# Block 6's first product by seven half-size products, first block's stores at once, another load order: a retention-plus-MLP kernel on one Trainium2 core

## The chip, the cores and the metric

The kernel runs on one core of a Trainium2 chip. Its time is device microseconds of one execution; lower is better. The engines are TensorE (PE in the profile, with its weight loads as PEld), VectorE (DVE), ScalarE (ACT), GpSimd (POOL) and SyncE (SP). Each works through its own instructions in order, and semaphores make one wait for another. POOL issues the loads (software queue, q0); SP issues the transposing DMAs and the stores (hardware queue, q1). Both queues are worked off by the same 16 DMA engines.

## The reference

```python
def _attn_ref(q, k, v):                      # (8, 8, 576, 64) each
    scores = scale * np.matmul(q, k.transpose(0, 1, 3, 2))
    gamma = 1.0 - 2.0 ** (-5.0 - np.arange(H))
    rel = pos[:, None] - pos[None, :]
    Dmat = np.where(rel >= 0, gamma[:, None, None] ** rel, 0.0)
    return np.matmul(scores * Dmat, v)
def _moe_ref(x, w_in, w_out):                # w_in 512 x 2048, w_out 2048 x 512
    h = x @ w_in
    g = 0.5 * h * (1.0 + erf(h * inv_sqrt2))
    return g @ w_out
# reference: x = attention's output, tokens first, 4608 x 512; then _moe_ref
```

There is no softmax, so the decay mask can be split into a factor of the row, a factor of the column and a running state between chunks of 128 positions.

## The kernel before, in words

**Attention.** The 8 batches are cut into chunks of 128 positions (the last has 64). One chunk of one batch is a unit of 128 tokens; there are 36 units in 22 groups (a group is two batches' units at the same chunk, or one unit of two 64-row tails; the first four groups are single units). In this text g4, g13, g17 and so on are groups by number; g7, g11, g16 and g21 are the short ones. For each group q and k are loaded with a cast to bf16, turned (q and k transposed), and then come: scores (`sc`, L507, L516, L526), a masked product on DVE (`ret`, L545, L549), `inner` (`o_ps`, L582, L591), `state` (`u_ps`, L610), `cross` (`o_ps` with `u_sb`, L642), and `evacuate` (L661), which writes the unit's tokens into `xT`. The first seven groups are turned by TensorE (L478); g7 to g21 by two transposing DMAs each on SP (`qkT<-qk_ld`, L489; `turn_dma`), one for q and one for k. TensorE's score matmuls of a group stand in its order and wait for both.

**MLP.** Nine blocks of 512 tokens, four units each. The first product (`mlp1`, `hT`, L690) of blocks 0 to 6 takes 64 matmuls of 128x128 on 512 columns per block; ACT applies Gelu (L699). The second product of block 0 is plain (`mlp2`, `oT`, L735); those of blocks 1 to 8 use seven half-size products instead of eight (`part`, `m`, L874, 112 matmuls of 256 columns per block), with sums on DVE (`sum_g`, L771 to L775) and combinations in `after`. Blocks 7 and 8 take seven products for the first product too (`fast`, `f`, L955, 112 matmuls of 256 columns): `sum_in` and `sum_last` (L913 to L920) make sums of `w_in` once, `sum_x` (L928) makes four sums of a block's `xT`, and each of the seven products goes through copies and additions on ACT and DVE (L452, L457, L970, L974) before Gelu (L976, L980).

**Order.** The order of all instructions is written at build time by a list scheduler inside the kernel: it keeps an estimated clock for each engine and for the two DMA queues and always issues the first piece whose inputs it believes ready. `ORDER` gives the load order of the first loads, and with it delays and choices found by search: `s20+3.0` keeps unit 20's group from being scored until 3.0 us after the believed landing of its transposes, `b6+0.3` does the same for `inner`, and `a8` puts the scaling of unit 8's v on ACT. Later loads follow group by group. `FAST` is the first block whose first product is done by seven products.

**Queues.** The four stores of block 0 are kept in `kept_back` and go out one at a time behind later transposes, from `HOLD` groups on:

```python
def store_kept():
    if kept_back and nD >= HOLD:
        store(*kept_back.pop(0))
```

`turn_dma` emits both transposes of a group when both its q and k are believed landed. POOL's loads are issued in order, at most eight in flight; a load waits also for its buffer (five pairs of q and k).

Of the kernel before, what the change touches and what calls it, by code (L numbers as in the profile page):

```python
# [17 lines left out]
def kernel(  # L18
# [14 lines left out]
    nc = tc.nc  # L33
# [19 lines left out]
    groups = [[0], [1], [2], [3]]  # L53
# [6 lines left out]
    N_U = len(units)  # L60
    group_of = {i: n for n, g in enumerate(groups) for i in g}
# [6 lines left out]

    N_PE_TR = 7
    HW_FIRST = ((("q", 0),), (("k", 0),))  # L70
    FAST, ALL_FAST = 7, 7
    N_LD = 5
    N_QKT = 4
    N_VH = 6
# [2 lines left out]
    A_TURNS = 2  # L77
    HOT = 5.3
    N_WARM = 10
    HOLD = 9  # L80

    const = ctx.enter_context(tc.tile_pool(name="const", bufs=1))
    ld_pool = ctx.enter_context(tc.tile_pool(name="ld", bufs=1))
# [176 lines left out]
    def hw_dma(issue, work, ready, put=lambda end: None, shares=TURN_SHARES):  # L260
        at = max(T["sp"], ready)
        if len(hw_flying) >= 3:
            T["sp"] = max(T["sp"], hw_flying[-3]["end"])
        T["sp"] = max(T["sp"], at + issue)
        hw_flying.append(transfer(1, at, work, put, shares))
# [59 lines left out]
    for x, keys in enumerate(zip(*HW_FIRST)):  # L325
        for n, (what, i) in enumerate(keys):
            land[what, i] = (4.6, 5.2)[n] + 0.75 * x
            t = tiles_of(i)
            cast_due[what, i] = (t[1] if what == "v" else t[0][:, "qk".index(what)], first[what, i])
    ORDER = ("wi1 q1 k1 wi0 io q2 k2 v0 v1 q3 wi2 v2 wi3 k3 wi4 v3 q4 wi5 wi6 q5 k4 a8 dq2 k5 wo1 wi7 wo0 v5 v4 "  # L330
# [4 lines left out]
             "b22+3.0 s23+2.0 s15+0.3 s13+3.0").split()  # L335

    BY_ACT = {int(x[1:]) for x in ORDER if x[0] == "a"}
    S_LATE = {int(x[1:].split("+")[0]): float(x.split("+")[1]) for x in ORDER if x[0] == "s"}
# [142 lines left out]
        release(b, done + 0.05)  # L481
        sg[n]["T"] = max(sg[n].get("T", 0.0), done + SEM)

    def turn_dma(n):
        qk, qkT = loaded[groups[n][0]][0], qkT_of(n)
        short = units[groups[n][0]][2] is None
        rows = TAIL if short else C
        for jj in range(2):
            nc.sync.dma_start(qkT[:, jj, :, 0:rows], qk[0:rows, jj].rearrange("p h j d -> p (h j d)"), transpose=True)  # L489
            ends = sg[n].setdefault("ends", {})  # L490

            def put(end, jj=jj):
                ends[jj] = end
                sg[n]["T"] = max(ends.values()) + SEM

            hw_dma(1.3, MOVE["turn"] * (0.62 if short else 1.0), max(land["qk"[jj], i] for i in groups[n]), put)

    def scores(n):
        g = groups[n]
# [215 lines left out]
    def store(t, ts, src, lo=0, hi=d_model, *on_queues):  # L715
        for x, (row, p0, n) in enumerate(rows_of(t, ts)):
            queue = on_queues[x] if on_queues else nc.sync
            queue.dma_start(out[row:row + n, lo:hi], src[p0:p0 + n])
        for _ in rows_of(t, ts):
            hw_dma(0.4, MOVE["store"] * (hi - lo) / d_model / len(rows_of(t, ts)), max(T["act"], T["dve"]), putter(o_free, (t, ts // 2)), STORE_SHARES)  # L720
# [7 lines left out]
    def mlp2(t, ts, m0, m1):  # L728
        cols = slice(ts * 128, ts * 128 + 128)
        if m0 == 0:  # L730
            acc[t, ts] = bank([128, d_model], FP32, "oT")
        b, oT = acc[t, ts]
        pe_waits(max(max(land_out[m // 2] + SEM, g_at[t, m, ts]) for m in range(m0, m1)))
        for m in range(m0, m1):
            nc.tensor.matmul(oT, lhsT=g_of(t, m // 2)[:, m % 2, cols], rhs=w_out_sb[m // 2][:, m % 2, :],  # L735
                             start=(m == 0), stop=(m == N_DF - 1))
        done = pe((m1 - m0) * 0.2158, m1 - m0)
        for m in range(m0 // 2, m1 // 2):
            begun["2", ts, m] = done
        if m1 == N_DF:  # L740
            if ts < 2:
                o_sb = tr_pool.tile([128, d_model], FP32, tag="qkT1", bufs=2, name="o")
            else:
                o_sb = const.tile([128, d_model], FP32, tag=f"qk{ts - 2}", name="o")
            nc.scalar.copy(o_sb, oT)
            release(b, on("act", 0.6, done) + SEM)
            kept_back.append((t, ts, o_sb))

    def store_kept():
        if kept_back and nD >= HOLD:  # L750
            store(*kept_back.pop(0))

    kept_back = []
    o_tiles, gs_tiles, gs_at = {}, {}, {}
    o_free = {}

# [142 lines left out]
    f_bank, f_at, f_done, f_begun, p7_tiles = {}, {}, {}, [], []  # L899

    def sum_in(mm):
        assert not kept_back
        w = w_in_sb[mm]
        a11, a12, a21, a22 = w[:, 0:2, 0:128], w[:, 2:4, 0:128], w[:, 0:2, 128:256], w[:, 2:4, 128:256]
        for x in range(3):
            n = 3 * mm + x
            if n // 4 not in wi_tiles:
                pool, tag = (const, f"qk{n // 4}") if n < 16 else (tr_pool, "qkT1")
                more = {} if n < 16 else {"bufs": 2}
                wi_tiles[n // 4] = pool.tile([128, 4, 2, 128], BF16, tag=tag, name=f"wi{n // 4}", **more)  # L910
            wi_sum[mm, x] = wi_tiles[n // 4][:, n % 4]
        s1, s2, s4 = (wi_sum[mm, x] for x in range(3))
        nc.vector.tensor_tensor(s1, a21, a22, op=ALU.add)  # L913
        nc.vector.tensor_tensor(s2, s1, a11, op=MINUS)
        nc.vector.tensor_tensor(s4, a12, s2, op=MINUS)
        wi_at[mm, 0] = on("dve", 0.85) + SEM
# [82 lines left out]
    def fast_ready(t, j, p):  # L999
        if any((t, n) not in xs_at for n in range(4)) or any((2 * j + x, y) not in wi_at for x in range(2) for y in range(2)):  # L1000
            return 1e9
        at = max([xs_at[t, {P7: 1, P6: 2, P4: 3}.get(p, 0)]] + [wi_at[2 * j + x, y] for x in range(2) for y in range(2)])
        if p == P1:
            if not may_begin(t, j):
                return 1e9
            if wanted[0] and lead()[0] == "3" and lead()[2] in (M3, M4, M1) or len(held) + 3 + pending() > 7:
                return 1e9
            if t >= ALL_FAST and nA < N_U and lead()[0] == "3":
                return 1e9
            if j == 2 and t < ALL_FAST and (t - 1, M1, 0) not in begun:  # L1010
                return 1e9
            return max(at, free_time(2))
        if p == P7:
            return max(at, free_time(1), f_at.get(((t, j - 2), "V"), f_at.get(((t - 1, j + 2), "V"), 0.0) if j < 2 else 1e9))
        at = max(at, f_at[(t, j), {P6: P1, P2: P1, P5: P6, P4: P6, P3: P5}[p]])
        return max(at, free_time(1)) if p == P6 else at
# [46 lines left out]
    def lead():  # L1063
        while runs and not (runs[0] and heads(runs[0])):
            runs.pop(0)
        one = heads(runs[0])[0][0] if runs else None
        return ("4", *one[1:]) if runs and kind_of(runs[0]) == "4" else one
# [53 lines left out]
    def fire():  # L1121
# [32 lines left out]
        while nV < N_U and nV < len(s_done) + N_VH and ("v", v_order[nV]) in land and ("v", v_order[nV]) not in cast_due:  # L1154
# [2 lines left out]
                break  # L1157
            scaled_v(i)
            nV += 1
        while (nD < len(groups) and nD < group_of[min(nX, N_U - 1)] + N_QKT  # L1160
               and all((what, i) in land and land[what, i] - 0.3 <= now for what in "qk" for i in groups[nD])):
            turn_dma(nD)
            nD += 1
            store_kept()

    def warm(n):
        b, t = bank([128, 512], FP32, "warm")
# [11 lines left out]
    while True:  # L1179
# [26 lines left out]
        if nB < nA:  # L1206
            if early:
                back = [nB]
            first_o = units[nB][1] == 0 and units[nB][2] == 0
            ready = max(max(st[i]["R"], land["v", i] if i in raw and nA < 8 else st[i].get("V", 1e9)) for i in back)  # L1210
            if any(("v", i) in cast_due for i in back):
                ready = 1e9
            ready = max(ready + B_LATE.get(back[0], 0.0), free_time(out_banks(back) + first_o))
            hurry = early or nA == N_U or stuck
            if not hurry and first:
                kind, t = first[0], first[1]
                hurry = nB < 4 * t + 4 if kind in "14" else len(runs[0]) <= (20 if t + 1 >= FAST else 6) and nB < 4 * t + 8
            if hurry:
                n = out_banks(back) + first_o + 2 * len(g)
                along = not early and nA >= 4 and scored <= now and len(frees(n)) == n and free_time(n) <= now + 0.3  # L1220
                cand(ready, "S", g if along else [], back)
# [68 lines left out]
        soon = [x for x in (land[key] for key in cast_due)] + [x[0] for x in queued] + [T["dve"] for x in queued]  # L1290
        if nV < N_U and ("v", v_order[nV]) in land and nV < len(s_done) + N_VH:
            soon += [land["v", v_order[nV]] + 0.1, T["dve"] - 1.9]
        if nD < len(groups) and all((x, i) in land for x in "qk" for i in groups[nD]):
            soon.append(max(land[x, i] for x in "qk" for i in groups[nD]) - 0.3)
        if wanted[0]:
            soon += [T["dve"] - 1.0 + 0.01]
        waits = [w for w in waits + soon if w > now and w < 1e8]
# [37 lines left out]
```

## Time and profile before

| | us |
|---|---|
| median of 3 runs (lowest, highest) | 286.8 (286.43, 288.02) |
| the profiled execution's own time | 288.85 |
| its span, first to last instruction | 287.1 |
| PE busy | 278.1 (97%) |
| DVE, ACT, POOL busy | 192.1, 153.2, 114.0 |
| load queue q0: share of 16 engines over the span | 93.7% |
| SP's queue q1: share of 16 engines over the span | 34.8% |
| granted TensorE clock | 1.00 throughout |

What lies outside the span is 288.85 - 287.1 = 1.75 us. The profiled execution was 2.05 us longer than the median of the three runs, so sums are made against 288.85 and 287.1 and then moved to 286.8. The page's second part cuts the span into 40 slices of 7.18 us; DMA engines are at nine tenths or more in the first 27 of them, to 194 us. The two shares of the DMA queues add up to more than 100% because packets of both queues overlap on an engine.

### The profile page before, as it was taken

How to read it: one execution, taken by the hardware profiler on the slowest of the kernel's cores; microseconds unless marked ns; L12 is line 12 of the kernel's file. 1: busy time of each engine (PE TensorE's matmuls, PEld its weight loads, DVE VectorE, ACT ScalarE, POOL GpSimd, SP SyncE). 2: the span in 40 equal slices, each digit the busy share in tenths (PEclk: the TensorE clock that was granted, in tenths of full speed). 3: DMA queues.
4: the chain of work that ended last, by engine and by line, in shares of the span. 5: the costliest groups of instructions: out<-in, count | busy, mean ns of one | idle time of the engine just before them, and what ended most of it. 6: DMA issues, size and time to landing. Idle time of an engine off the chain costs nothing.

```text
span 287.1 us, 7914 instructions
## 1 busy us (share of the span) xinstructions
PE 278.1 (97%) x3310; PEld 202.3 (70%) x3310; DVE 192.1 (67%) x400; ACT 153.2 (53%) x346; POOL 114.0 (40%) x143
## 2 busy tenths in 40 slices
PE   7989999999999999899999999999999999999994
PEld 2568677578864688348855686468755888888893
DVE  4834682789865795788098817673589659966922
ACT  4956436664549524773258438872566363565320
POOL 8997888995245355325667434100000000000000
PEclk9999999999999999999999999999999999999999
DMA  9999999999999999999999999990220000400234
GB/s 144 169 178 184 187 182 156 142 124 128 159 153 249 157 134 127 156 196 147 167 177 165 147 135 138 219 103 1 75 75 0 2 0 2 146 2 1 75 110 112
DMA packets 152803, 35.38 MB, mean 123 GB/s; under 512 B 141120, under 2 KB 148928, under 8 KB 152768
## 3 DMA queue, kind: packets, MB, share of 16 engines
q0 software_dynamic: 116832, 18.10, 93.7%
q1 hardware_dynamic: 34528, 16.26, 34.8%
q10 hardware_dynamic: 1408, 0.52, 0.7%
q8 instruction: 26, 0.43, 0.6%
q14 instruction: 9, 0.07, 0.1%
HBM read 36.70 MB, written 9.44 MB: 161 GB/s over the span
## 4 chain that ended last, share of the span: by engine, by line
PE 76%; DMA 16%; POOL 4%; DVE 2%; issue 1%; POOLq 0%; SPq 0%
PE m L874 28%; PE hT L690 26%; PE f L955 9%; DMA qk_ld<-in_q_dram 5%; PE oT L735 5%; DMA qk_ld<-in_k_dram 4%; DMA qkT<-qk_ld 4%; DMA qk<-in_k_dram 3%; PE o_ps L591 2%; PE sc L526 2%; POOL qk L318 2%; PE qk_ps L478 1%; POOL w_in L291 1%; PE u_ps L610 1%; PE o_ps L642 1%; POOL v_ld L318 1%
## 5 line engine op out<-in xcount | busy, mean ns | idle before, releaser
L690 PE MATMUL hT<-xT,w_in 128*128 128x512 bf16 (+3 forms) x624 | 101.7, 319 | 0.0
L699 ACT ACTIVATE g<-hT 128x512 bf16<-128x512 f32 (+2 forms) x121 | 66.2, 564 | 41.6 <-PE hT L690 41.1
L690 PEld LDWEIGHTS <-w_in 128*128 128x128 bf16 x624 | 54.7, 98 | 39.9
L874 PEld LDWEIGHTS <-gs 128*128 128x128 bf16 x656 | 62.3, 98 | 7.6
L874 PE MATMUL m<-w_sum,gs 128*128 128x256 bf16 (+1 forms) x400 | 46.8, 268 | 0.1
L318 POOL DMA_DIRECT2D v_ld<-in_v_dram x40 | 34.1, 860 | 22.3 <-DMA qk_ld<-in_k_dram 11.3
L549 DVE TENSOR_TENSOR ret<-sc,msk 128x512 bf16<-128x512 f32 x48 | 30.2, 682 | 15.2 <-PE sc L526 15.0
L318 POOL DMA_DIRECT2D qk_ld<-in_k_dram x36 | 30.3, 850 | 23.1 <-DMA qk_ld<-in_q_dram 21.0
L318 POOL DMA_DIRECT2D qk_ld<-in_q_dram x36 | 30.6, 855 | 19.2 <-DMA qkT<-qk_ld 5.4
L874 PE MATMUL m<-w_out,gs 128*128 128x256 bf16 x256 | 32.2, 273 | 0.0
L874 PE MATMUL m<-w_sum,g 128*128 128x256 bf16 x256 | 30.6, 273 | 0.0
L563 ACT ACTIVATE vh<-v_ld,dv 128x64 bf16<-128x64 bf16 x112 | 27.9, 337 | 0.0
L874 PEld LDWEIGHTS <-g 128*128 128x128 bf16 x256 | 25.1, 98 | 4.0
L771 DVE TENSOR_TENSOR gs<-g 128x1024 bf16<-128x1024 bf16 x32 | 21.7, 686 | 7.6 <-ACT g L699 7.4
L661 DVE TENSOR_TENSOR xT<-o_ps,dqT 128x512 bf16<-128x512 f32 (+1 forms) x32 | 18.4, 616 | 5.4 <-PE o_ps L642 5.1
L775 DVE TENSOR_TENSOR gs<-g 128x1024 bf16<-128x1024 bf16 x32 | 21.4, 682 | 0.0
L457 ACT COPY o<-m 128x512 f32<-128x512 f32 x14 | 8.2, 585 | 22.8 <-PE m L874 22.8
L826 DVE SCALAR_TENSOR_TENSOR o<-m,o 128x512 f32<-128x512 f32 (+1 forms) x9 | 5.6, 629 | 18.7 <-PE m L874 10.1
L980 ACT ACTIVATE g<-f 128x512 bf16<-128x512 f32 x24 | 13.6, 591 | 6.9 <-PE f L955 6.9
L457 ACT CAST u_sb<-u_ps 128x512 bf16<-128x512 f32 x14 | 8.2, 585 | 16.4 <-PE u_ps L610 16.4
L735 PE MATMUL oT<-w_out,g 128*128 128x512 bf16 x64 | 15.5, 380 | 0.0
L549 DVE TENSOR_TENSOR ret<-sc,near 128x512 bf16<-128x512 f32 x16 | 10.3, 683 | 7.2 <-PE sc L526 6.0
(96 smaller groups left out, 303.9 us busy)
## 6 DMA issues: line engine op xcount, KB each, us to landing
out_dram<-o SPq DMA_DIRECT2D x27, 256.0 KB, 7.1
v_ld<-in_v_dram POOLq DMA_DIRECT2D x32, 128.0 KB, 8.9
qk_ld<-in_q_dram POOLq DMA_DIRECT2D x28, 128.0 KB, 9.6
qk_ld<-in_k_dram POOLq DMA_DIRECT2D x28, 128.0 KB, 10.7
w_in<-in_moe_w_in_dram POOLq DMA_DIRECT2D x8, 256.0 KB, 6.8
w_out<-in_moe_w_out_dram POOLq DMA_DIRECT2D x8, 256.0 KB, 8.2
out_dram<-o SPq DMA_DIRECT2D x14, 128.0 KB, 2.3
qk_ld<-in_k_dram POOLq DMA_DIRECT2D x8, 64.0 KB, 9.6
```

The lines of the kernel that those rows point to most:

```text
L318: nc.gpsimd.dma_start(dst, src[2 * bp + jj, :, ci * C:ci * C + n, :].rearrange("h s d -> s h d"))
L457: nc.scalar.copy(dst, src)
L549: nc.vector.tensor_tensor(r, t, by, op=ALU.mult)
L563: nc.scalar.activation(vh[:, h, :], loaded[i][1][:, h, :], AF.Copy, scale=dv[:, h, ci:ci + 1])
L661: nc.vector.tensor_tensor(x_of(i)[:, :, n * x:n * x + n], o, dqT[:, :, ci * C:ci * C + n], op=ALU.mult)
L690: nc.tensor.matmul(hT[:, m, :], lhsT=w[:, cc, o:o + 128], rhs=x_tiles[t][:, cc, lo:hi], start=(cc == 0), stop=(cc == N_DM - 1))
L699: nc.scalar.activation(g_of(t, m0 // 2)[:, m0 % 2:m0 % 2 + n, lo:hi], hT, AF.Gelu)
L735: nc.tensor.matmul(oT, lhsT=g_of(t, m // 2)[:, m % 2, cols], rhs=w_out_sb[m // 2][:, m % 2, :], start=(m == 0), stop=(m == N_DF - 1))
L771: nc.vector.tensor_tensor(s.rearrange("p m a b -> p m (a b)"), g[:, :, 0, :], g[:, :, 1, :], op=ALU.add)
L775: nc.vector.tensor_tensor(s, g[:, :, :, LEFT], g[:, :, :, RIGHT], op=MINUS)
L874: nc.tensor.matmul(m[:, 0 if apart else ts, :], lhsT=a, rhs=w[:, c0:c1], start=p in begins and mm == 0 and ts == 0, stop=mm == N_DF // 2 - ...
L955: nc.tensor.matmul(m[:, y, :], lhsT=a[:, c], rhs=d[:, c], start=p in (P1, P7) and y == 0 and c == 0, stop=c == 1, skip_group_check=True)
```

## The change

`FAST` and `ALL_FAST` go from 7 to 6: block 6's first product takes seven half-size products. A condition that kept such a product from beginning while attention was unfinished is gone. Block 0's stores are issued as soon as their results are copied out. `turn_dma` emits the transpose of q and that of k separately, each when its own loads are believed landed. `ORDER` is another: load order, delays (`s`, `b`) and choices (`a`). The limits of "hurry", by which the scheduler pulls `inner` forward, change.

```diff
-    FAST, ALL_FAST = 7, 7
+    FAST, ALL_FAST = 6, 6
...
-    HOLD = 9
...
-    ORDER = ("wi1 q1 k1 wi0 io q2 k2 v0 v1 q3 wi2 v2 wi3 k3 wi4 v3 q4 wi5 wi6 q5 k4 a8 dq2 k5 wo1 wi7 wo0 v5 v4 "
-             "wo3 wo2 q6 wo6 q8 dq3 wo7 v7 wo4 k6 k7 wo5 q7 v6 v9 v11 k9 q9 k8 k10 s4+0.6 q10 k11 k12 v8 q12 a29 "
-             "v10 dq4 s31+0.6 s27+6.0 a27 a6 a20 q11 v12 a28 a7 s34+4.0 a19 b6+0.3 b21+1.5 b7+2.0 s21+3.0 b10+4.0 "
-             "s8+0.6 s11+0.3 b17+2.0 s32+6.0 b19+6.0 s2+0.3 b23+1.0 b18+1.0 s18+1.0 a13 s16+0.3 a11 s20+3.0 "
...
+    ORDER = ("wi0 wi1 k1 io q1 q2 v0 v1 k2 k3 q3 wi2 v2 wi3 k4 a28 v3 wi4 wi5 q5 wi6 a34 q4 k5 wo0 v4 wo1 wi7 v5 "
+             "wo2 wo3 q6 wo5 q8 wo6 v7 dq2 wo7 dq3 q7 wo4 k10 k7 k6 v6 k8 q9 k9 q10 v8 v11 q11 v9 v10 k12 b3+0.3 "
+             "q12 s8+0.3 a26 dq4 s0+1.5 v12 a32 a30 a29 s9+1.5 s11+1.0 a27 k11 s29+2.0 s13+0.3 a6 s26+3.0 b14+2.0 "
...
-    def turn_dma(n):
+    def turn_dma(n, jj):
...
+    def turnable(now):
+        if nD >= len(groups) or nD >= group_of[min(nX, N_U - 1)] + N_QKT:
+            return None
+        return next((jj for jj in range(2) if jj not in sg[nD].get("ends", {})
+                     and all(("qk"[jj], i) in land and land["qk"[jj], i] - 0.3 <= now for i in groups[nD])), None)
...
-            kept_back.append((t, ts, o_sb))
-
-    def store_kept():
-        if kept_back and nD >= HOLD:
-            store(*kept_back.pop(0))
+            store(t, ts, o_sb)
...
-            if t >= ALL_FAST and nA < N_U and lead()[0] == "3":
-                return 1e9
...
-                hurry = nB < 4 * t + 4 if kind in "14" else len(runs[0]) <= (20 if t + 1 >= FAST else 6) and nB < 4 * t + 8
+                hurry = nB < 4 * t + 4 if kind in "14" else len(runs[0]) <= (8 if t + 1 >= FAST else 16) and nB < 4 * t + 8 + 4 * (t + 1 >= FAST)
```

More of the change, by code (lines that the diff above doesn't have):

```diff
@@ L329 @@
             cast_due[what, i] = (t[1] if what == "v" else t[0][:, "qk".index(what)], first[what, i])
-    ORDER = ("wi1 q1 k1 wi0 io q2 k2 v0 v1 q3 wi2 v2 wi3 k3 wi4 v3 q4 wi5 wi6 q5 k4 a8 dq2 k5 wo1 wi7 wo0 v5 v4 "
[4 rows of a table removed]
-             "b22+3.0 s23+2.0 s15+0.3 s13+3.0").split()
+    ORDER = ("wi0 wi1 k1 io q1 q2 v0 v1 k2 k3 q3 wi2 v2 wi3 k4 a28 v3 wi4 wi5 q5 wi6 a34 q4 k5 wo0 v4 wo1 wi7 v5 "
[4 rows of a table added]
+             "s35+1.5 b18+2.0 b8+1.0 s33+0.6 a10 b23+0.6 b9+0.6 s7+2.0 b19+0.6 s14+1.5 b12+6.0 b13+0.3 s15+0.3").split()
     BY_ACT = {int(x[1:]) for x in ORDER if x[0] == "a"}
@@ L487, in turn_dma, with put @@
         rows = TAIL if short else C
[L488 to L496, printed above, removed]
+        nc.sync.dma_start(qkT[:, jj, :, 0:rows], qk[0:rows, jj].rearrange("p h j d -> p (h j d)"), transpose=True)
+        ends = sg[n].setdefault("ends", {})
+        def put(end):
+            ends[jj] = end
+            sg[n]["T"] = max(ends.values()) + SEM
+        hw_dma(1.3, MOVE["turn"] * (0.62 if short else 1.0), max(land["qk"[jj], i] for i in groups[n]), put)
+    def turnable(now):
[3 more added lines that the diff above has]
+                     and all(("qk"[jj], i) in land and land["qk"[jj], i] - 0.3 <= now for i in groups[nD])), None)
     def scores(n):
@@ L746, in mlp2 @@
             release(b, on("act", 0.6, done) + SEM)
-            kept_back.append((t, ts, o_sb))
-    def store_kept():
-        if kept_back and nD >= HOLD:
-            store(*kept_back.pop(0))
-    kept_back = []
+            store(t, ts, o_sb)
     o_tiles, gs_tiles, gs_at = {}, {}, {}
@@ L901, in sum_in @@
     def sum_in(mm):
-        assert not kept_back
         w = w_in_sb[mm]
@@ L1159, in fire @@
             nV += 1
[L1160 to L1164, printed above, removed]
+        while True:
+            jj = turnable(now)
+            if jj is None:
+                break
+            turn_dma(nD, jj)
+            nD += len(sg[nD]["ends"]) == 2
     def warm(n):
@@ L1292 @@
             soon += [land["v", v_order[nV]] + 0.1, T["dve"] - 1.9]
-        if nD < len(groups) and all((x, i) in land for x in "qk" for i in groups[nD]):
-            soon.append(max(land[x, i] for x in "qk" for i in groups[nD]) - 0.3)
+        if nD < len(groups):
+            for x in "qk":
+                if all((x, i) in land for i in groups[nD]):
+                    soon.append(max(land[x, i] for i in groups[nD]) - 0.3)
         if wanted[0]:
```

3 rows, old and new, of the table ORDER are left out of this document.

## The prediction

> **What bounds the kernel now.** I read the page's busy shares and slices first, then the engine waits, the chain of waits in order of time, the groups of the transposing DMAs, and the timeline of PE, DVE and POOL.
>
> ```profile
> PE 278.1 (97%) x3310; PEld 202.3 (70%) x3310; DVE 192.1 (67%) x400; ACT 153.2 (53%) x346; POOL 114.0 (40%) x143
> ...
> PE   7989999999999999899999999999999999999994
> ...
> DMA  9999999999999999999999999990220000400234
> ```
>
> PE is never free for long, so the time is PE's work plus its few waits. But the DMA engines are full until 194 us too: attention's loads and transposes are a second line that PE must not overtake. Where it does, it waits:
>
> ```profile
> PE sc L526 <- DMA qkT<-qk_ld: 1.7, 1, 1.7
> PE qk_ps L478 <- DMA qk<-in_k_dram: 1.2, 1, 1.2
> ```
>
> The first wait is the one that matters. The chain of waits shows its place, and the pace of PE's work around it (start, us, what):
>
> ```profile
> 97.90 12.86 DMA qk_ld<-in_k_dram
> ...
> 110.81 11.45 DMA qkT<-qk_ld
> ...
> 122.30 0.64 PE sc L526 x32
> ...
> 178.09 8.74 PE hT L690 x40
> ...
> 192.00 11.35 PE m L874 x104
> ...
> 223.94 0.87 PE f L955 x8
> ```
>
> At 122.30 PE scores g13. Its last load of k was issued at 97.90 and landed at 110.76, the transpose was issued at once and took 11.45 us to 122.26; PE had been there since 120.6. From the third fence I take 8.74/40 = 0.2185 us for 512 columns, 11.35/104 = 0.1091 and 0.87/8 = 0.109 for 256.
>
> **Block 6's first product.** It loses 64 x 0.2185 = 13.98 us and gets 4 x 7 x 4 = 112 x 0.1091 = 12.22: 1.77 us less PE work. One clearing matmul (`mark`) of 0.22 is new. Steady PE work: -1.55. Two more filler matmuls at the start (0.43) fill idle time and cost nothing.
>
> A rule speaks against this step. The Trainium skill's page "TensorE: Matmul & The Clock Gate", section "Back-to-back issue gap", gives sustained spacings that grow far less than the columns do (81 ns at 128 columns, 131 ns at 512), so halving the columns would not halve the cost. An estimate from these two figures, about 98 ns at 256, would make it 112 x 0.098 = 11.0 against 64 x 0.131 = 8.4: 2.6 us more work instead of 1.77 less. The rows disagree: 0.109 against 0.2185 is a half.
>
> On the other engines the changed order holds on DVE 8 more additions (L970, L974) x 0.69, 4 more `sum_x` x 0.415, and with copies and the other edits 18 more instructions, 11.6 us (192 to 204); on ACT 4 us more. In the stretch where block 6's seven products run (39 us of PE work) the changed order has some 42 DVE instructions, 27 us or 70%; before, from 220 to 260 us, where blocks 7's and 8's ran, DVE was busy 29.55 of 40 us and PE waited for nothing. So I count zero; the cover is the second product of the block before, woven in by 0.44 or 0.87 us as before.
>
> **Start.** The new load order brings v0 forward by one 128 KB load: 0.9 us (loads land 0.87 us apart here; v0 landed at 12.12). k3, which PE waited for until 19.37 (1.2 us), is now tenth instead of thirteenth, but v3 (20.8 by its place) takes over a wait of some 1.0. Followed load by load, PE reaches the scores of g4 at 28.95 instead of 29.91: -0.96, of uncertain size (-2 to +0.6).
>
> **Up to g13.** In the changed order PE has 89.09 us of work between the scores of g4 and of g13, before 89.53. With 1.1 us of small gaps as before it stands at g13 at 28.95 + 89.09 + 1.1 = 119.15, before at 120.6. When do the transposes land? Loads up to g13's k are the same set, and so are transposes up to g13 and the stores (blocks 0 and 1, eight) that go before. Only their order differs: block 0's four stores landed at 75.99, 84.30, 90.84 and 99.14, each after a transpose; now three go between g7's two transposes and the fourth behind them, at about 57. From 61 to 133 us every load was issued within 1.0 us after the landing of the one eight places earlier, so the load queue never ran dry. What is full conserves its work: the stores' 0.9 us each is paid earlier, and g13's k lands at about 110.8 again, its transpose at about 122.3. Then PE waits 3.1 us instead of 1.7 and the start's gain is gone. `s20+3.0`, which held g13's scores back in the plan, is absent now, so the plan puts them no later than the old one did.
>
> The Trainium skill says the same from the other side: "DMA: Bandwidth & Descriptors", section "Issuing engines are not separate DMA queues", has all issuers on the same 16 engines, interleaved. By it moving a store from one stretch to another frees nothing, and the stores' edit is worth 0. Against it, rows: with both queues busy two transposes landed 3.4 us apart around 78 to 90, but 6.4 and 5.1 around 110 to 122, so the shares change. No row bounds the new landing exactly; I take 122.3, with 118 (all four stores' spacing of 0.9 to 2.4 us gained) and 124 as ends.
>
> **After g13.** Both programs leave g13's scores at the same instant; PE work left is 159.89 instead of 160.56: -0.67. The next tight place is g17. It was scored 7.2 us after its transposes had landed (164.43); now it comes 41.67 instead of 49.34 us of work behind g13, 7.7 earlier. Its transposes stand on SP behind block 3's stores, which wait for DVE's subtraction (L840, 148.35 to 149.03, itself behind two `vh` multiplications, now one: -0.6). From block 3's last product (144.77) to the landing were 19.66 us, now some 19.05; PE's work between the two is 18.45. That is a wait of 0.6 by this profile, whose second transpose took 11.5 us, the longest of thirty:
>
> ```profile
> DMA to landing us min/median/max: 3.8/9.9/11.5
> ```
>
> With the median there is none: 0.3 taken, ends 0 and 2.9. g18 and g19 keep 2 to 3 us (6.1 and 8.2, less 3.9 and 5.3). g20 comes 14.0 earlier and had 13.1, but its transposes now stand on SP ahead of block 4's five stores (175.88 to 179.41), which gives 3 us or more back. g21's scores come 7 us of work later and wait for nothing. The tail after the last first product is the same 16 to 17 us of `m` and stores. POOL's `dqT` steps (about 1 us each) move among loads that are issued 4 to 9 us ahead of their landing: nothing. The separate transposes of q and k shorten waits in SP but not the second landing, which PE needs: nothing.
>
> **Sum.** -0.96 start, -1.11 work from g4 on (-1.77, +0.22 `mark`, +0.44 done later), +1.4 longer wait at g13, +0.3 at g17: -0.4 us. So the profiled execution would be 288.85 - 0.4 = 288.4 and the median 286.8 - 0.4 = 286.4. If the runs without a profile have a shorter wait at g13 (their median is 2.05 us lower), both programs lose the same part of it, down to 120.6.
>
> **Rivals.** (1) *Transposes come earlier too.* Without block 0's stores in between, the chain of transposes g8 to g10 is shorter and g13's land before 119. Then the waits go: -0.96 - 1.11 - 1.7 + 0.3 = -3.5, 283.3 us. For it: each of these stores held up the queue by 0.9 to 2.4 us. Against: the full load queue. (2) *Attention becomes the bound to its end, slower than before.* g13's wait as forecast, and g17's transposes land 2.9 us after PE's arrival at about 164.0, since g18's loads share the engines with them: -0.67 + 2.9 = +2.2, 289.0. It ends over 0.5% slower when that wait passes 2.1 us. For it: margins of g17 to g20 fall from 6 to 13 us to under 3; against: the 11.5 us already taken is the maximum. (3) *Block 6's steps wait for DVE.* Sixteen hand-overs (four column groups, four each) with one DVE instruction of 0.69 us ahead, less the 0.44 us of cover: 16 x 0.25 = 4.0, so +3.6: 290.4. Against: no such wait in the blocks that do it now. (4) *Half-wide products are not half as dear.* If weight loads of 98 ns showed fully, 112 instead of 64 are 4.7 us more: +4.3, 291.1; the row of 0.109 speaks against it (this is what the page's figures would amount to). That the change does what it says is seen in its order: block 6's products begin before g21's scores.
>
> **Numbers.** Half a percent, 1.43 us, is about what a measurement of this kernel can tell from no change: 285.4 to 288.2. Chances: forecast 0.46, rival (1) 0.26, (2) 0.19, (3) 0.08, (4) 0.01. The forecast's own range, with the ends at g13 and g17, is 284.9 to 287.9: 0.38 same, 0.06 faster, 0.02 slower. Of (1) 0.24 is faster, 0.02 same; (2) to (4) are slower. Together 0.30 faster, 0.40 same, 0.30 slower. The 8-in-10 range runs from rival (1) to just above (2): 283.2 to 289.3.
>
> **What would show it.** PE's `f` group at 336 instructions from 224 and `hT` 512-wide at 264; a wait of about 3 us of the scores L530 for `qkT<-qk_ld` near 119 to 122, landing within 1.5 us of 122.3; a second one under 1 us near 164; no PE wait from 187 us of work on. No wait at g13 makes rival (1) right; waits summing to over 5 us after 150 make (2) or (3) right; PE's products at other than 0.109 make (4) right.

## The result, and the profile after

| | before | after |
|---|---|---|
| median (lowest, highest), 18 runs each | 286.81 (286.22, 288.02) | 288.06 (287.15, 289.58) |
| ratio, 95% interval | 1 | 1.0042 [1.003, 1.0055] |
| profiled execution, its span | 288.85, 287.1 | 288.88, 287.1 |
| PE, DVE busy | 278.1, 192.1 | 276.5, 204.8 |
| PE, DVE busy, profile repeated | 279.3, 192.6 | 278.0, 205.2 |

The change costs 1.2 us. The forecast was 0.4 us less than before. The two profiled executions are equally long, which hides the difference: the one of before was 2.0 us above its median, the one of after only 0.8.

The page of after, busy shares and slices (the columns are those of the prediction's first fence):

```profile
PE 276.5 (96%) x3333; PEld 207.0 (72%) x3353; DVE 204.8 (71%) x418; ACT 156.8 (55%) x362; POOL 114.2 (40%) x143
...
PE   8899989999999999999999899999999999999994
...
DMA  9999999999999999999999999990002100400133
```

Against the 3353 weight loads, 20 matmul records are missing here (3333); the repeated profiles, with all of them, have PE busy for 278.0 us, before for 279.3. So PE has some 1.3 us less to do (its busy time in one and the same program varies by as much: 278.1 and 279.3 for before), near the forecast, and nothing of it shows in the time. The engine waits of after say what took its place (us in total, times, longest):

```profile
PE o_ps L595 <- DVE vh L570: 1.5, 1, 1.5
PE sc L530 <- DMA qkT<-qk_ld: 1.3, 1, 1.3
```

The wait for `vh` is new. The wait of the scores is not the one of before: the chain of waits (start, us, what) has it at g17, 164 us, and has no wait at g13 at all.

```profile
130.36 11.35 PE m L873 x104
...
151.46 12.44 DMA qkT<-qk_ld
...
233.86 2.18 PE f L953 x20
```

The second transpose of g17, issued at 151.46, took 12.44 us. Half-wide products cost what the prediction gave them: 11.35/104 = 0.1091 for `m`, 2.18/20 = 0.109 for `f`. The same chain, asked for 28 to 39 us, shows the new wait. From 30.46 to 37 us the end is set by DVE, where the chain of before had nothing but PE:

```profile
30.46 1.88 DVE ret L553 x3
32.34 0.20 DVE w_sum L191
32.54 1.91 DVE w_sum L192
34.44 0.20 DVE w_sum L193
34.65 1.70 DVE w_sum L194
36.35 0.61 DVE vh L570
36.96 0.04 issue
37.00 0.41 PE o_ps L595 x8
```

Two `w_sum` additions of 0.2 to 0.4 us took 1.9 and 1.7. `vh` stands behind them on DVE, and PE's `inner` of g4 behind `vh`. The timeline of DVE, with the tile shapes, and below it that of POOL (start, us):

```profile
32.26 0.28 DVE L191 TENSOR_TENSOR w_sum<-w_out 128x256 bf16<-128x256 bf16 x1
32.45 1.99 DVE L192 TENSOR_TENSOR w_sum<-w_out 128x256 bf16<-128x256 bf16 x1
34.37 0.28 DVE L193 TENSOR_TENSOR w_sum<-w_out 128x256 bf16<-128x256 bf16 x1
34.57 1.78 DVE L194 TENSOR_TENSOR w_sum<-w_out 128x512 bf16<-128x512 bf16 x1
```

```profile
33.23 1.05 POOL L298 TENSOR_TENSOR dqT<-dqT,step 128x512 f32<-128x512 f32 x1
34.22 0.76 POOL L304 DMA_DIRECT2D w_out<-in_moe_w_out_dram  x1
35.00 1.05 POOL L298 TENSOR_TENSOR dqT<-dqT,step 128x512 f32<-128x512 f32 x1
```

The two long additions end 0.16 and 0.30 us after POOL's two `dqT` steps end (34.28 and 36.05). That is in both cases 0.12 us less than the addition takes alone (0.28 and 0.42). So I read that each stood still until POOL's step was all but over and then ran. The traces of all runs bear this out: 14 `w_sum` or `vh` instructions overlap a `dqT` step and end after it, and each ends 0.12 to 0.13 us sooner than the step's end plus its own time. Lines 191 and 193, of the same kind, took 0.28. In the changed load order both `dqT` steps lie there. In the kernel before, POOL's timeline has them at 18.59, when DVE was idle, and here:

```profile
30.93 1.05 POOL L299 TENSOR_TENSOR dqT<-dqT,step 128x512 f32<-128x512 f32 x1
```

DVE's timeline of before has beside that step four products `ret`, which read one tile from PSUM, and they were not held: 2.48/4 = 0.62 us each, as elsewhere.

```profile
30.54 2.48 DVE L549 TENSOR_TENSOR ret<-sc,msk 128x512 bf16<-128x512 f32 x4 [1.78 <-PE sc L526]
32.95 0.28 DVE L192 TENSOR_TENSOR w_sum<-w_out 128x256 bf16<-128x256 bf16 x1
33.14 0.28 DVE L193 TENSOR_TENSOR w_sum<-w_out 128x256 bf16<-128x256 bf16 x1
```

The Trainium skill has this as a rule, on the page "SBUF — State Buffer", section "Who interferes with whom": a DVE instruction with two SBUF inputs contends with a GpSimd instruction that reads SBUF, the one issued second waits for the whole of the other, and one with at most one SBUF input, outside the 2-port perf modes, does not contend. The rows agree on who contends: `w_sum` (two SBUF inputs) took 1.99 instead of 0.28 and 1.78 instead of 0.42, `ret` (one) 0.62 as ever. Which was issued second they do not show: by the recorded starts `w_sum` was 0.78 and 0.43 us ahead of the step that held it. The rule was not used in the prediction.

### The profile page after: what moved, and what is told of

It reads as the page before. It is cut to its first block, busy times and chain, and to the rows that moved or that the text cites. A ratio compares the mean times of both kernels' runs of the same rounds, so it can differ in the third digit from the quotient of the medians.

```text
span 287.1 us, 8042 instructions
## 1 busy us (share of the span) xinstructions
PE 276.5 (96%) x3333; PEld 207.0 (72%) x3353; DVE 204.8 (71%) x418; ACT 156.8 (55%) x362; POOL 114.2 (40%) x143
## 4 chain that ended last, share of the span: by engine, by line
PE 87%; DMA 6%; DVE 2%; POOL 2%; issue 1%; POOLq 0%; SPq 0%
PE m L873 34%; PE hT L694 25%; PE f L953 13%; DMA qkT<-qk_ld 4%; PE oT L739 4%; PE o_ps L595 3%; PE sc L530 3%; DMA v_ld<-in_v_dram 2%; PE u_ps L614 1%; PE qk_ps L477 1%; PE o_ps L646 1%; POOL qk L317 1%; DVE w_sum L192 1%; DVE ret L553 1%; DVE w_sum L194 1%
## 5 line engine op out<-in xcount | busy, mean ns | idle before, releaser
L694 PE MATMUL hT<-xT,w_in 128*128 128x512 bf16 (+3 forms) x539 | 86.4, 313 | 0.6
L703 ACT ACTIVATE g<-hT 128x512 bf16<-128x512 f32 (+2 forms) x105 | 57.3, 559 | 28.1 <-PE hT L694 26.8
L694 PEld LDWEIGHTS <-w_in 128*128 128x128 bf16 x552 | 48.4, 98 | 33.1 <-DMA w_in<-in_moe_w_in_dram 0.3
L873 PE MATMUL m<-w_sum,gs 128*128 128x256 bf16 (+1 forms) x400 | 48.2, 268 | 0.0
L317 POOL DMA_DIRECT2D v_ld<-in_v_dram x40 | 34.0, 854 | 27.0 <-DMA qk_ld<-in_k_dram 10.9
L873 PE MATMUL m<-w_out,gs 128*128 128x256 bf16 x256 | 33.0, 273 | 0.0
L567 ACT ACTIVATE vh<-v_ld,dv 128x64 bf16<-128x64 bf16 x128 | 31.8, 340 | 0.0
L978 ACT ACTIVATE g<-f 128x512 bf16<-128x512 f32 x36 | 20.6, 591 | 11.1 <-PE f L953 10.0
L953 PEld LDWEIGHTS <-w_in 128*128 128x128 bf16 x192 | 18.8, 98 | 2.3
L456 ACT CAST u_sb<-u_ps 128x512 bf16<-128x512 f32 x15 | 8.8, 586 | 19.5 <-PE u_ps L614 19.5
L974 ACT ACTIVATE g<-p 128x512 bf16<-128x512 f32 x12 | 7.6, 630 | 19.3 <-DVE p L972 19.3
L456 ACT COPY o<-m 128x512 f32<-128x512 f32 x13 | 7.6, 586 | 16.6 <-PE m L873 16.6
```

The lines of the kernel that those rows point to most:

```text
L317: nc.gpsimd.dma_start(dst, src[2 * bp + jj, :, ci * C:ci * C + n, :].rearrange("h s d -> s h d"))
L456: nc.scalar.copy(dst, src)
L567: nc.scalar.activation(vh[:, h, :], loaded[i][1][:, h, :], AF.Copy, scale=dv[:, h, ci:ci + 1])
L694: nc.tensor.matmul(hT[:, m, :], lhsT=w[:, cc, o:o + 128], rhs=x_tiles[t][:, cc, lo:hi], start=(cc == 0), stop=(cc == N_DM - 1))
L703: nc.scalar.activation(g_of(t, m0 // 2)[:, m0 % 2:m0 % 2 + n, lo:hi], hT, AF.Gelu)
L873: nc.tensor.matmul(m[:, 0 if apart else ts, :], lhsT=a, rhs=w[:, c0:c1], start=p in begins and mm == 0 and ts == 0, stop=mm == N_DF // 2 - ...
```

## Experiments

The theory: (A) POOL's two `dqT` steps, moved beside DVE instructions with two SBUF inputs, delay `vh` and cost 1 to 1.5 us; (B) g17's transposes, behind block 3's four stores on SP, now come too late for PE; block 6's products themselves gain. The rivals: block 6's products, or the denser attention, cost the time. For the trace I use one number throughout: the time at which PE starts the scores of a group, less the PE work that stands before it in the kernel's order (counted at the spacings above, 0.2185 us for 512 columns and 0.1091 for 256). It grows only where PE stands idle. I call it PE's lost time.

**The kernel before, again** (no edit).

> The kernel before once more, for a second profile. Theory one (the profile of before was a slow execution): its 1.7 us wait of the scores at 122 us for transposes is short or gone, the span is 285 to 286 us. Theory two (the wait is regular): 1.5 to 2 us at the same place and a span near 287.

It took 286.76 us, span 285.0. The chain passes g13 without a wait; its transposes landed at 119.15, not 122.26. In a second repetition with the last group of runs:

> The kernel before a third time: as r_before, no wait at g13 (landing 118.5 to 121, PE there at 120.6), span 284.5 to 286.

It took 287.19 us, span 285.3; g13's transposes landed at 117.94, 2.5 us ahead of PE. So the wait of 1.7 us on which the prediction built belonged to one execution. Lost time at PE's end was 7.50 and 7.28 us, in the first profile 9.16.

**(A) taken away, first try: `dqT` steps earlier.** In the changed kernel POOL's first two `dqT` steps (numbers 2 and 3 in the code) go ahead of the loads q4 and q8:

```diff
+    DQ_AT = {"q4": 2, "q8": 3}
...
+        if what + str(i) in DQ_AT:
+            dq_step(DQ_AT[what + str(i)])
```

> The kernel after, with POOL's first two dqT steps issued earlier (ahead of the loads q4 and q8, while VectorE idles or reads PSUM); all other engines' orders are unchanged. Theory one (port and start): w_sum at L192 and L194 is back at 0.28 and 0.42 us instead of 1.99 and 1.78, PE's 1.5 us wait for vh near 35 us is gone, and 0.6 to 1.5 us of it reaches the end (ratio to before 0.999 to 1.002), the rest turning into waits at transposes, whose margins were 0.6 to 1.1 us at g8 to g10 and g13. Theory two (transposes set the pace, a loss at the start is taken up later): the wait for vh is gone, but waits for transposes grow by as much and the ratio stays at 1.004.

Median 287.38, ratio to before 1.0019 [1.0, 1.0038]. The `w_sum` additions took 0.28 and 0.42 again and the wait at 35 us was gone. But the first step, now at 17.48, met another multiplication with two SBUF inputs. DVE's timeline, POOL's, and the engine waits of this run:

```profile
17.02 2.18 DVE L580 TENSOR_TENSOR vh<-v_ld,dv 128x512 bf16<-128x512 bf16 x1
```

```profile
17.48 1.17 POOL L288 TENSOR_TENSOR dqT<-dqT,step 128x512 f32<-128x512 f32 x1
```

```profile
PE u_ps L624 <- DVE vh L580: 0.9, 1, 0.9
```

This `vh` needs 0.68 alone. It ended at 19.20, which is the step's end (18.65) plus 0.55, again 0.13 less than its own time. The second step, beside `ret`, cost nothing. The hold followed the step to its new place: a miss as a repair, and the best evidence for the cause.

**(B) taken away: block 3's stores behind g17's transposes.** In the changed kernel, `store` keeps the four stores of block 3 and they go out after the second transpose of g17:

```diff
+            while nD == 17 and jj == 1 and kept3:
+                store_now(*kept3.pop(0))
```

> The kernel after, with block 3's four stores issued on SP behind g17's two transposes instead of ahead of them; all else unchanged. Theory one (the stores' place makes g17 late): g17's transposes land before 160 us, PE's 1.3 us wait there is gone and 0.8 to 1.3 us reaches the end (ratio 0.9995 to 1.0015). Theory two (the full load queue makes it late): they land within 1 us of 163.9, or g18 or g20 waits instead, ratio 1.003 to 1.005.

Median 287.67, ratio 1.0025 [1.0012, 1.0038]: 0.4 us better than after, which the two intervals do not tell apart, and less than the 0.8 to 1.3 expected. g17's transposes landed at 152.97, 9.6 us ahead of PE, and only the other wait was left:

```profile
PE o_ps L595 <- DVE vh L570: 1.4, 1, 1.4
```

**Both edits together.**

> Both edits. Theory one: the gains add, 1.5 to 2.7 us less than the kernel after, ratio 0.995 to 0.999. Theory two: waits only move to the transposes of g8 to g13 and g18 to g20, ratio 1.002 to 1.004.

Median 287.07, ratio 0.9999 [0.9987, 1.0012]. That is 1.0 us better than after, where 1.5 to 2.7 were expected. The wait for the `vh` at 17 us remained (1.1), so this was not yet the clean case.

**(A) put into the kernel before.** Its load order is untouched; only the two steps go later, ahead of the loads wo7 and wo4:

```diff
+    DQ_AT = {"wo7": 2, "wo4": 3}
```

> The kernel before, with POOL's first two dqT steps issued ahead of the loads wo7 and wo4, so that they meet w_sum and vh on VectorE near 33 to 36 us as in the kernel after; all else unchanged. Theory one (a step on POOL holds up VectorE instructions that read two tiles from SBUF, and PE's loss reaches the end): two of L192 to L195 or L566 take 1 us or more longer each, PE waits 1 to 2.5 us for vh at g4's inner, and the time rises by 0.7 to 2 us, ratio 1.0025 to 1.007. Theory two (a loss at the start is taken up by waits later): the same wait, ratio 0.999 to 1.002.

Median 287.63, ratio 1.0015 [0.9998, 1.0033], 0.7 us above before. The interval alone does not settle it, and the ratio lies below the 1.0025 to 1.007 expected: only one of the two steps met an addition. DVE's timeline, and POOL's:

```profile
32.83 0.79 DVE L192 TENSOR_TENSOR w_sum<-w_out 128x256 bf16<-128x256 bf16 x1
...
33.95 1.25 DVE L195 TENSOR_TENSOR w_sum<-w_out 128x512 bf16<-128x512 bf16 x1
```

```profile
33.77 1.15 POOL L289 TENSOR_TENSOR dqT<-dqT,step 128x512 f32<-128x512 f32 x1
```

One `w_sum` took 1.25 instead of 0.42, ending 0.28 after the second step. Another took 0.79 instead of 0.28, with no `dqT` step recorded beside it; a third, at 53.17, took 0.61 in the same way. I can't explain these two. PE's lost time was 0.8 us more at g5 than in the repeated kernel before (7.35 against 6.56), and still 0.8 more at g13 (8.24 against 7.43) and at the end (8.31 against 7.50). In this trace a wait this early is carried to the end unchanged. The first step, which fell beside `ret`, was free again.

**Block 6's products undone in the changed kernel.**

```diff
-    FAST, ALL_FAST = 6, 6
+    FAST, ALL_FAST = 7, 7
```

> The kernel after with FAST = ALL_FAST = 7: block 6's first product plain again, everything up to g17 in the same order. PE work in the order is 1.55 us more. Theory one (the seven products pay in full): 1.2 to 1.9 us more than the kernel after, ratio to before 1.008 to 1.011. Theory two (they lose at hand-overs what they save): ratio 1.003 to 1.006.

Median 289.38, ratio 1.0082 [1.0054, 1.011]: 1.3 us worse than after, of 1.55 us more PE work. Block 6's products gain, nearly in full, in the changed order. That ends the rival that they cost the time; the denser attention is not tested by this run.

**Block 6's products alone, in the kernel before.** `FAST, ALL_FAST = 6, 6`, and the condition on unfinished attention taken out, as in the change.

> The kernel before with FAST = ALL_FAST = 6 and the condition on unfinished attention gone, its load order, stores and limits kept. PE work in the order is 1.76 us less. Theory one (the seven products pay in full): ratio 0.9925 to 0.996. Theory two (they lose at hand-overs or at attention's last transposes what they save): ratio 0.998 to 1.003.

Median 287.35, ratio 1.0015 [0.9996, 1.0034]: no gain, although PE's work is 1.76 us less. Here PE waits between seven-product steps. The engine waits, and PE's timeline at the longest of them:

```profile
PE f L955 <- DVE xs L928: 0.7, 1, 0.7
...
PE f L955 <- ACT g L980: 0.3, 1, 0.3
PE f L955 <- ACT f L457: 0.2, 1, 0.2
```

```profile
247.49 0.61 PE L955 MATMUL f<-xs,w_in 128*128 128x256 bf16 x4 [0.74 <-DVE xs L928]
```

Between 224 and 248 us PE stood idle for 1.9 us in four places, about half of it for DVE and half for ACT. None of them is in block 6: its 112 `f` products run from 192.67 to 215.97, those of block 7 begin at 223.44 and those of block 8 at 246.14. What this order did move is the end of attention: g21's scores come at 234.34 instead of 213.60, and block 8's sums `xs` stand on DVE at 246.7 to 248 us, when PE is there already. Lost time grew from 7.66 at g19 to 10.19 at the end; in after only from 9.90 to 10.15. So block 6's seven products met no wait here either. Whether the later end of attention makes the waits of blocks 7 and 8 no run tests.

**(A) and (B) taken away, `dqT` steps where DVE is idle.** As both edits together, but the first step ahead of load v4, at about 21 us:

```diff
-    DQ_AT = {"q4": 2, "q8": 3}
+    DQ_AT = {"v4": 2, "q8": 3}
```

> As e3_both, but POOL's first dqT step ahead of the load v4, near 21 us, where VectorE has nothing to do (in e1 and e3 it stretched a vh from 0.68 to 2.18 us). Theory one (PE's loss reaches the end): vh is back at 0.68 us, PE's wait of 0.9 to 1.1 us for it gone, 0.4 to 0.9 us less than e3_both, ratio 0.9965 to 0.9985; what does not arrive is found as waits at g8 to g13, whose margins were 0.26 to 0.85 us in e3_both. Theory two (transposes set the pace from here): as e3_both within 0.2 us, ratio 0.999 to 1.001.

Median 286.70, ratio 0.9991 [0.9973, 1.001], just above the 0.9965 to 0.9985 expected; again in the last group of runs:

> e7_dq_idle once more, for the interval and for a second profile: ratio 0.997 to 1.000; if runs without a short wait are typical, PE ends near 280 us again; if its median lies above its profile because transposes are often later, this profile shows 0.3 to 1 us of waits at g8 to g10 or g13, whose margins were 0.2 to 1.0 us.

Median 286.72, ratio 0.9986 [0.997, 1.0001]. Beside it, on the same chip, the changed kernel once more:

> The kernel after once more, on the same chip as e7: ratio 1.003 to 1.0055, so e7 1.0 to 1.7 us below it. The wait of 1.4 us for vh at 35 us comes again within 0.2 us; that for g17's transposes (1.3 us in the first profile) lies between 0 and 1.5 us, by the edit of e2 0.4 us on average.

Median 288.0, ratio 1.0037 [1.0022, 1.0053]. So this version is 1.3 us faster than after, with intervals that do not overlap. Against before, 0.1% is not told apart from nothing. In the first of its two profiles no engine wait but the start's was left; DVE's timeline has the additions at their own length, and POOL's has the step where DVE stood idle (20.6 to 22 us):

```profile
32.61 0.29 DVE L192 TENSOR_TENSOR w_sum<-w_out 128x256 bf16<-128x256 bf16 x1
...
33.01 0.42 DVE L194 TENSOR_TENSOR w_sum<-w_out 128x512 bf16<-128x512 bf16 x1
```

```profile
20.90 1.05 POOL L288 TENSOR_TENSOR dqT<-dqT,step 128x512 f32<-128x512 f32 x1
```

In the second profile g13's transposes landed at 120.46 instead of 119.27 and PE waited for them:

```profile
PE sc L540 <- DMA qkT<-qk_ld: 0.7, 1, 0.7
```

The repeated profile of after had the wait for `vh` again (1.3 us) but none at g17, whose second transpose took 10.9 us instead of 12.4 and landed 0.17 us ahead of PE. The wait for `vh` is part of the order of the program; the one at g17 comes and goes with the transfers.

**Block 0's stores held back again.** The version above, with those four stores one at a time behind the transposes of g8 to g11:

```diff
+            if nD in (8, 9, 10, 11) and len(sg[nD]["ends"]) == 2:
+                store_now(*kept0.pop(0))
```

> As e7_dq_idle, but block 0's four stores go out one at a time behind the transposes of g8, g9, g10 and g11, as in the kernel before. Theory one (the DMA engines are full, so a store's place only moves its cost): g7's and g8's transposes land 1 to 3 us earlier than in e7, those of g10 to g13 within 1 us of where they did, and the time is that of e7 within 0.3 us. Theory two (stores at once are what the change gains at g9 to g13): those land 1.5 us or more later, PE waits there 0.5 to 2 us, ratio 1.001 to 1.005.

Median 286.9, ratio 0.9997 [0.9978, 1.0015], beside 0.9986 of the same version with the stores at once: not told apart. Landing of the second transpose, from the records of the DMA queue:

| group | stores at once (two profiles) | held back |
|---|---|---|
| g7 | 61.78, 62.08 | 59.38 |
| g8 | 74.82, 74.71 | 73.73 |
| g9 | 81.50, 81.81 | 81.23 |
| g13 | 119.27, 120.46 | 120.48 |

With the stores at once the transposes land some 2.5 us later at g7, 1.0 at g8 and 0.4 at g9, and no later at g13. This is one profile of the held version, in which PE reached g4 about 1 us late, after a wait of 1.1 us for a load of `w_in` at 26.9 that the edit does not touch.

## Why the prediction was wrong

The sum's terms, against the profile of after less the repeated profile of before (PE ends at 282.81 and 281.27, +1.54), and against differences of medians where an experiment isolates one:

| term | forecast | in the profiles | in medians |
|---|---|---|---|
| start, scores of g4 | -0.96 | -0.78 | |
| PE work from g4 on | -1.11 | -1.11 | -1.3 for block 6's products, forecast -1.55 |
| `dqT` steps on POOL | 0 | +1.7 | +1.0 |
| wait at g13 | +1.4 | 0 | |
| wait at g17 | +0.3 | +1.4 | +0.4 |
| small gaps of PE | 0 | +0.3 | |
| sum | -0.4 | +1.5 | +1.2 for the change |

The 1.0 of the medians is 287.67 (block 3's stores moved) less 286.70 (the `dqT` steps moved as well), whose intervals do not overlap; the 0.4 is 288.06 less 287.67, whose intervals do. The profiled execution of after had a longer wait at g17 than its repetition, hence in part the larger sum. Not all of the 1.7 for the steps arrives at the end either: against the profile with only the stores moved (281.46), PE ends 1.5 and 0.5 us earlier in the two profiles without the hold, and in the second of them it waits 0.7 us at g13 instead.

**The step that failed** is the sentence "POOL's `dqT` steps (about 1 us each) move among loads that are issued 4 to 9 us ahead of their landing: nothing." It followed the moved instruction on its own engine and on the DMA queue behind it, where no cost showed. It did not look at what stood beside it on DVE. The changed order shows the steps' new place among the loads; DVE's timeline of before shows `w_sum` and `vh`, both with two SBUF inputs, from 33 us on. This one term is larger than the distance between forecast and no change, and with it and the stores put right the same kernel is back at the time of before.

**The term at g13 was mis-sized, in its base.** "Both programs lose the same part of it" (in the forecast's sum, for the runs without a profile) took a wait of one execution as a property of the program. The landing varied from 117.9 to 122.3 in three profiles of before and from 119.3 to 120.8 in the nine with the changed order. In both repetitions of before, at 286.76 and 287.19 us close to the median, there was no wait to lengthen, and none for an earlier start to be eaten by. The prediction's own test, "no wait at g13 makes rival (1) right", thus failed: the wait was absent without rival (1)'s gain of 1.7 us, for it was absent in the repetitions of before too. The range for this landing, 118 to 124, did hold it.

**The term at g17 had its mechanism right**: PE arrives earlier by block 6's postponed work, and the transposes stand behind block 3's stores. The prediction took 0.3 with a PE arrival at about 164.0 and a transpose of at most 11.5 us. PE arrived at 162.6, as it had not waited at g13, and the transpose took 10.9 to 12.4; hence 0 to 1.3. Rival (2) described this wait but did not reach its threshold of 2.1 us.

**What held.** The 336 `f` products, counted by form in the trace of after (count, total, mean ns):

```profile
L953 PE MATMUL f<-xs,wi 128*128 128x256 bf16 x96 | 14.4, 272 | 0.0
L953 PE MATMUL f<-xT,w_in 128*128 128x256 bf16 x96 | 14.2, 273 | 0.0
...
L953 PE MATMUL f<-xs,w_in 128*128 128x256 bf16 x96 | 14.1, 273 | 0.0
...
L953 PE MATMUL f<-xT,wi 128*128 128x256 bf16 x48 | 7.2, 273 | 0.0
```

They cost half a full-width product each, so the sustained spacings of the Trainium skill's page "TensorE: Matmul & The Clock Gate", section "Back-to-back issue gap", which spoke against the step, were rightly set aside. DVE's 11.6 us more work (10 measured, 202.6 against 192.6 where nothing is held) cost PE nothing in block 6, as forecast, and not in the run with block 6 alone either. Rival (3) put its wait of 4.0 us at block 6's steps; such waits exist in that run, 1.9 us, but in blocks 7 and 8. Issuing block 0's stores at once left the landing at g13 where it was within its spread, as argued from the full load queue. The start came out at -0.78 against -0.96 (-0.4 to -0.8 over the pairs of profiles).

**What stays open.** The version with both causes taken away keeps 1.1 us less PE work and about 0.5 us of the start (g4 at 29.4 to 29.6 against a mean of 29.9 before), yet its median is only 0.1 to 0.2 us below before (0.3 to 0.4 by the ratios). That this comes out near the forecast's -0.4 is luck: the sum came to it with a wait at g13 longer by 1.4, and the two profiles have 0 and 0.7 there. In its two profiles PE ends 1.2 and 0.2 us earlier than the mean of the repeated ones of before (281.16). The second has the wait at g13, and in both PE comes within 1 us of the landing at g8, g9, g10 and g13, where the repeated profiles of before had 1.5 to 8.4 us. That the rest, about 1 us, is lost in such waits as the transfers vary, which is the rival of the denser attention, fits, but no run separates it.

## What to carry to other kernels

When a step moves on GpSimd, look at what lies beside it on VectorE: if it reads SBUF there and VectorE's instruction has two SBUF inputs, VectorE's may stand still until the step is over, and everything queued behind it too. Such steps belong beside instructions that read PSUM, or into an idle stretch. A wait for a transfer in a single profile is one draw: take a second profile of the same kernel before giving it a share in a sum, and price it by its margin and the spread of the landing.

## What the runs showed of the hardware

A DVE addition with two SBUF inputs that needs 0.28 us took 1.99 beside a POOL `tensor_tensor` of 1.05 us. Its record begins 0.78 us before that of POOL's step and ends 0.16 us after it, so the loss exceeds the length of the step. POOL's step itself took 1.05 there, and 1.15 to 1.19 in three other cases. Once it was POOL's that stood: in the run with both edits its third step, of half the width, took 1.11 us instead of some 0.66, beside a `vh` whose record begins 0.09 us earlier and which took 0.74 instead of 0.68. POOL's DMA issues alone did not hold `w_sum` or `vh`: over all 14 traces 618 of 620 that ran beside an issue and no `dqT` step kept their own time, and the other two are the unexplained ones above. One and the same transposing DMA took 12.4 and 10.9 us in two executions of one program, issued at the same time within 0.03 us.
